# Alternating the last mixture products of a fused recurrence and mixer between two PSUM banks

## The chip, the cores and the metric

The kernel runs on one core of one Trainium2 chip. The metric is the device time of one execution in microseconds (us), from the profiler on the chip. A core has five engines with a queue of instructions each: TensorE (PE: matmuls, their weight loads are PEld), VectorE (DVE), ScalarE (ACT), GpSimd (POOL) and SyncE (SP, which here issues nearly all DMAs). Each engine takes its own queue strictly in order and waits for the others through semaphores. Matmuls write to PSUM, which has eight banks of 2 KB per partition; DVE and ACT read it.

## What is computed

A recurrence over 768 steps for 4 batches of 8 heads, and a gated mixer over its output:

```
for t in range(S):                                   # S = 768, state 40 x 40 per head
    y[t]  = r[t] @ state
    Sa    = state @ a[t]
    state = state * w[t] - outer(Sa, b[t]) + outer(v[t], k[t])
x = y as [batch, S, 320]
h = relu(x @ w_in)                                   # 320 -> 1024
u, v = h[..., :512], h[..., 512:]
v_n = (v - mean(v)) / sqrt(var(v) + 1e-6)
v_s = einsum('ts,bsd->btd', w_spatial, v_n) + b_spatial[:, None]
out = (u * v_s) @ w_out                              # 512 -> 320
```

## The kernel before

There are two phases in one program. **Phase 1** goes through the recurrence in NS = 24 chunks: two pairs of batches (bq = 0, 1) with twelve chunks of 64 steps each. Every chunk has a chain of small matmuls (c_bp L535, c_ff L553, c_xx L571, c_mp L603, c_y L627) with ACT copies and POOL masks between them, and every fourth chunk gets the inverses of its blocks from `invert`, whose temporary, itmp, is a PSUM tile that DVE writes and reads. Each second chunk ends with 128 finished steps stored to the DRAM buffer xs.

Beside the recurrence phase 1 computes `relu(x @ w_in)`. For each of twelve tiles j (a pair of batches and 128 steps) it loads x (`m_load`, L670 and L674), splits it into two float32r parts xh and xl (`m_split`: ACT, then POOL L54) and runs six **products** of eight matmuls each: four of `m_u` (L739; a slice of u for both batches, 128x256) and two of `m_v` (L694; the v half for one batch, 128x512). ACT takes each product out of PSUM with the Relu (L741 for u, L696 for v). u goes to the DRAM buffer uts. v is normalised first (`m_n1`, `m_root`, `m_n2`, `m_n3`: DVE, POOL, ACT) and then goes to vns. I number the products k = 0 to 71 in the program's order; every third (50, 53, ..., 71) is an `m_v`. The tiles xh, xl, ur and vr have two buffers each. All products use one PSUM tile, pv, in the pool ps_m with one buffer.

**Phase 2** is the mixer over the steps. For each batch b and each half h of its steps, `spatial(b, h)` makes four PSUM tiles pg (d = 0 to 3; 18 matmuls each, L173 to L175); DVE adds the bias (L177) and multiplies by u (L178, tile ut, loaded from uts at L158), and ACT and POOL split the result into gh and gl. `proj` multiplies these by w_out: three tiles po of 12 matmuls (L193), one half behind `spatial`. The tiles gh, gl and g have two buffers, pg has four, po three. The buffers vh, vl of v (loaded at L149 into raw) and ut alternate between two sets; the set for b = 1 and 3 lies in SBUF where phase 1's xh, xl, ur and vr lie.

The order: `plan` is a list of pieces with due times in chunks, and the part before time 24 is written in this order under manual_schedule. The pieces from time 24 on, which I call the **tail** (products 52 to 71), and all of phase 2 are put in order by the framework's scheduler, which sets them between each other and the last chunks. So the order on each queue is fixed when the program is built.

Of the kernel before, what the change touches and what calls it, by code (L numbers as in the profile page):

```python
# [8 lines left out]
F32 = mybir.dt.float32  # L9
# [6 lines left out]
PSUM = bass.MemoryType.PSUM  # L16
DRAM = bass.MemoryType.DRAM

P = 128
# [4 lines left out]
NB = 2  # L24
# [7 lines left out]
DH = 512  # L32

@with_exitstack
def tile_kernel(ctx, tc, early, late, vtok, win, wspT, bsp, wout, out):
    nc = tc.nc
    dram = ctx.enter_context(tc.tile_pool(name="dram", bufs=1, space=DRAM))
    B = out.shape[0]
    S = out.shape[1]
    xs = dram.tile([B, 2, NP, E, S], F32, name="xs")  # L40
    vns = dram.tile([B, S // P, P, DH], F32, name="vns")
    uts = dram.tile([B // NB, S // P, DH // P, P, NB, P], F32, name="uts")
    with ExitStack() as c1:
        phase1(c1, tc, early, late, vtok, win, xs, vns, uts, dram)
    with ExitStack() as c2:
        phase2(c2, tc, vns, uts, wspT, bsp, wout, out)
# [165 lines left out]
def phase1(ctx, tc, early, late, vtok, win, xs, vns, uts, dscr):  # L212
    nc = tc.nc
    NS = early.shape[1]
# [6 lines left out]
    def pool(name, bufs=1, **kw):  # L221
        return ctx.enter_context(tc.tile_pool(name=name, bufs=bufs, **kw))
# [10 lines left out]
    moe = pool("moe")  # L233
    ps_k = pool("ps_k", 2, space=PSUM)
    ps_c = pool("ps_c", 2, space=PSUM)
    ps_i = pool("ps_i", 1, space=PSUM)
    ps_b = pool("ps_b", 1, space=PSUM)
    ps_m = pool("ps_m", 1, space=PSUM)

    warm = const.tile([P, 1], F32, name="warm")  # L240
# [442 lines left out]
        split_lo(LO_ENG, xh[64:, 2], xt[64:, 2], xh[64:, 2])  # L683
        st["xhl", key] = (xh, xl)

    def m_v(g, bq, i):
        xh, xl = st["xhl", (bq, i)]
        pv = ps_m.tile([P, DH], F32, name="pv")
        vc = slice(DH, 2 * DH)
        mm = [(xh[:, k, g, :], wh[:, k, vc]) for k in range(3)]  # L690
        mm += [(xh[:, k, g, :], wl[:, k, vc]) for k in range(3)]
        mm += [(xl[:, k, g, :], wh[:, k, vc]) for k in range(2)]
        for j, (l, r) in enumerate(mm):
            nc.tensor.matmul(pv, lhsT=l, rhs=r, start=(j == 0), stop=(j == len(mm) - 1))  # L694
        vr = st["act"].tile([P, DH], F32, name="vr", bufs=2)
        nc.scalar.activation(vr, pv, AF.Relu)  # L696
        st["vr", g] = vr
# [30 lines left out]
        nc.scalar.activation(vr, vr, AF.Identity, bias=q[:, 2:3], scale=q[:, 1:2])  # L728
        nc.sync.dma_start(out=vns[bq * NB + g, i], in_=vr)

    def m_u(d, bq, i):
        xh, xl = st["xhl", (bq, i)]
        dc = slice(d * P, (d + 1) * P)
        pu = ps_m.tile([P, NB, P], F32, name="pv")
        mm = [(wh[:, k, dc], xh[:, k]) for k in range(3)]
        mm += [(wh[:, k, dc], xl[:, k]) for k in range(2)]
        mm += [(wl[:, k, dc], xh[:, k]) for k in range(3)]
        for j, (l, r) in enumerate(mm):
            nc.tensor.matmul(pu, lhsT=l, rhs=r, start=(j == 0), stop=(j == len(mm) - 1))  # L739
        ur = st["act"].tile([P, NB, P], F32, name="ur", bufs=2)  # L740
        nc.scalar.activation(ur, pu, AF.Relu)  # L741
        nc.sync.dma_start(out=uts[bq, i, d], in_=ur)
# [4 lines left out]
    def at(t, fn, *args):  # L747
        plan.append((t, len(plan), fn, args))
# [4 lines left out]
    v, p = nc.vector, nc.gpsimd  # L753
# [48 lines left out]
    for q in range(GS, NS):  # L802
        t = PREP.get(q, q - 8 + 0.01)
# [20 lines left out]
            at(T_DEC + i + k * 0.12 - (0.9 if k == 0 else 0), step, gen)  # L824
    at(T_DEC + 5.9, open_act)
    slots = [T_MOE + k // 4 + (M1, M2, M3, M4)[k % 4] for k in range(3 * NS)]
    for j in range(NS // 2):
        bq, i = j // 6, j % 6
        own = slots[6 * j:6 * j + 6]
        at(max(own[0] - 1.6, 2 * j + 2.1, T_DEC + 5.92), m_load, bq, i)  # L830
        at(max(own[0] - 0.7, 2 * j + 2.7), m_split, bq, i)
        for t, d in zip((own[0], own[1], own[3], own[4]), range(DH // P)):
            at(t, m_u, d, bq, i)
        for t, g in zip((own[2], own[5]), range(NB)):
            at(t, m_v, g, bq, i)
            at(t + 0.14, m_n1, g)
            at(t + 0.42, m_root, g)
            at(t + 0.48, m_n2, g)
            at(t + 0.76, m_n3, g, bq, i)
# [12 lines left out]
    with tc.manual_schedule():  # L852
# [77 lines left out]
        while plan[n][0] < NS:  # L930
            t, _, fn, args = plan[n]
# [59 lines left out]
```

## Time and profile before

| | us |
|---|---|
| median of three runs | 725.92 (725.43 to 728.48) |
| profiled execution, its own time | 728.03 |
| profiled execution, span from first to last instruction | 726.2 |
| PE busy in the span | 592.8 (82%) |
| DVE, ACT, POOL busy | 448.6, 415.1, 289.7 |

The page gives the mean granted clock of PE as 0.901 of full speed. In the page's 40 slices of 18.2 us PE is at nine tenths or more from the 23rd slice to the 39th, but for the 26th with an 8 and the 35th with a 5. The matmul groups at L173, L174 and L175 (pg) have 192 matmuls each and the longest busy times of PE, 65.1, 65.0 and 64.8 us.

How to read it: a busy share is a mean over stages with different bounds. So the windows of the end of the program are read apart, and for each the question is which wait ended last there.

### The profile page before, as it was taken

Reading aid. Unit: us, or ns where it says so; the run is one execution under the profiler, and the core shown is the slowest. Engines: PE = TensorE matmul, PEld = TensorE weight load, DVE = VectorE, ACT = ScalarE, POOL = GpSimd, SP = SyncE. Lnnn points to the kernel's source line nnn. Section 1 sums busy time; section 2 is a strip of 40 time slices with the busy share of each in tenths; the row PEclk is TensorE's granted clock in tenths of the full one; section 3 lists DMA queues with packets and bytes.
Section 4 is the critical chain, followed back from the end, with each engine's and each line's share of the span. In section 5 each row is a group of like instructions: output and inputs, shape, how many; then the busy total and the mean of one; then the engine's idle time right before and its main releaser. Section 6 shows DMA issues by size and latency. Waiting matters only on the chain. (4 is left out here: it accounts for less than half of the span.)

```text
span 726.2 us, 25447 instructions
## 1 busy us (share of the span) xinstructions
PE 592.8 (82%) x10784; PEld 535.0 (74%) x10784; DVE 448.6 (62%) x884; ACT 415.1 (57%) x904; POOL 289.7 (40%) x486
## 2 busy tenths in 40 slices
PE   2707776587776877989988999899999999599997
PEld 1606665586665776868877788788789998499997
DVE  7898689968999998758797565311247201343221
ACT  2406763377655666878878798798754423332112
POOL 4102230124433435354554543464549822373221
PEclk9956997578977888989999999999899999799999
DMA  9443675294444535454365344344263533650001
GB/s 186 86 90 69 104 145 112 51 185 94 106 91 101 112 82 118 112 126 112 102 187 165 85 133 127 106 120 116 73 198 108 158 108 100 189 180 34 28 28 55
DMA packets 101337, 81.35 MB, mean 112 GB/s; under 512 B 33576, under 2 KB 90152, under 8 KB 99304
## 3 DMA queue, kind: packets, MB, share of 16 engines
q1 hardware_dynamic: 100680, 78.01, 43.3%
q10 hardware_dynamic: 544, 1.72, 1.1%
q8 instruction: 85, 1.39, 0.9%
q14 instruction: 28, 0.23, 0.1%
HBM read 59.20 MB, written 20.50 MB: 110 GB/s over the span
## 5 line engine op out<-in xcount | busy, mean ns | idle before, releaser
L396 POOL TENSOR_SCALAR_AFFINE_SELECT Rt<-Rt 64x512 f32<-64x512 f32 (+1 forms) x144 | 84.1, 585 | 102.2 <-ACT Rt L582 74.4
L545 ACT ACTIVATE Rt<-bp 64x416 f32<-64x416 f32 x96 | 49.1, 512 | 68.2 <-PE bp L535 66.4
L351 DVE TENSOR_TENSOR itmp<-A 128x30 f32<-128x30 f32 (+9 forms) x180 | 73.7, 409 | 3.3
L396 POOL TENSOR_SCALAR_AFFINE_SELECT At<-At 64x512 f32<-64x512 f32 x48 | 36.9, 768 | 94.6 <-ACT At L406 92.5
L173 PE MATMUL pg<-wsh,vh 128*128 128x384 f32 x192 | 65.1, 339 | 0.0
L174 PE MATMUL pg<-wsl,vh 128*128 128x384 f32 x192 | 65.0, 339 | 0.0
L175 PE MATMUL pg<-wsh,vl 128*128 128x384 f32 x192 | 64.8, 337 | 0.0
L355 DVE TENSOR_TENSOR A<-A,itmp 128x30 f32<-128x30 f32 (+9 forms) x180 | 59.0, 328 | 6.2
L535 PE MATMUL bp<-lin,Mc 40*64 40x104 f32 x768 | 53.1, 301 | 11.1 <-DVE y L640 10.3
L535 PEld LDWEIGHTS bp<-lin,Mc 40*64 40x64 f32 x768 | 46.2, 167 | 16.0 <-DVE y L640 13.4
L177 DVE TENSOR_TENSOR g<-pg,bb 128x384 f32<-128x384 f32 x32 | 17.7, 553 | 63.9 <-PE pg L175 56.9
L702 DVE BATCH_NORM_STATS2 bs<-vr 128x6 f32<-128x512 f32 x24 | 16.6, 690 | 60.3 <-ACT vr L696 60.2
L54 POOL TENSOR_TENSOR gl<-g,gh 128x384 fp32r<-128x384 f32 x32 | 33.8, 1062 | 47.7 <-ACT gh L50 47.7
L582 ACT ACTIVATE Rt<-ch 64x416 f32<-64x416 f32 x96 | 49.2, 512 | 3.9 <-PE ch L571 1.5
L326 PE MATMUL bk<-at,sl 64*32 64x32 f32 x1536 | 24.4, 221 | 28.6 <-DVE sl L313 14.5
L553 PE MATMUL ch<-Rt,At 128*64 128x104 f32 x768 | 46.0, 277 | 1.2 <-issue 1.2
L50 ACT ACTIVATE gh<-g 128x384 fp32r<-128x384 f32 x32 | 16.7, 522 | 52.3 <-DVE g L178 52.3
L441 PE MATMUL bk<-ident,sl 128*128 128x128 f32 x192 | 31.7, 297 | 17.4 <-ACT tk L447 6.9
L553 PEld LDWEIGHTS ch<-Rt,At 128*64 128x64 f32 x768 | 40.3, 152 | 5.7 <-issue 3.0
L326 PEld LDWEIGHTS bk<-at,sl 64*32 64x32 f32 x1536 | 20.6, 132 | 30.7 <-DVE sl L313 14.6
L571 PE MATMUL ch<-ffs,xf 64*64 64x104 f32 x768 | 42.6, 263 | 0.0
L54 POOL TENSOR_TENSOR vl<-raw,vh 128x512 fp32r<-128x512 f32 x24 | 32.1, 1350 | 25.8 <-ACT vh L50 24.8
(121 smaller groups left out, 1604.2 us busy)
## 6 DMA issues: line engine op xcount, KB each, us to landing
ein<-in_early SPq DMA_DIRECT2D x40, 387.0 KB
lin<-in_late SPq DMA_DIRECT2D x48, 160.0 KB
uts<-ur SPq DMA_DIRECT2D x48, 128.0 KB
vns<-vr SPq DMA_DIRECT2D x24, 256.0 KB
raw<-vns SPq DMA_DIRECT2D x24, 256.0 KB
ut<-uts SPq DMA_DIRECT2D x24, 256.0 KB
Rt<-in_vtok SPq DMA_DIRECT2D x48, 80.0 KB
xs<-y SPq DMA_DIRECT2D x48, 80.0 KB
```

Source lines behind the costliest of these rows:

```text
L54: eng.tensor_tensor(out=lo, in0=x, in1=hi.bitcast(F32), op=ALU.subtract)
L173: nc.tensor.matmul(pg, lhsT=vh[:, dc], rhs=w_h, start=(i == 0), stop=False)
L174: nc.tensor.matmul(pg, lhsT=vh[:, dc], rhs=w_l, start=False, stop=False)
L175: nc.tensor.matmul(pg, lhsT=vl[:, dc], rhs=w_h, start=False, stop=(i == NT - 1))
L326: nc.tensor.matmul(pl[o:o + HB, n, :], lhsT=sl[PR[par], n, par, cs], rhs=at[PR[par], n, cs], start=True, stop=True,)
L351: nc.vector.tensor_tensor(out=tp, in0=A[:, k + 1:, k:k + 1].broadcast_to([P, m, k]), in1=A[:, k:k + 1, 0:k].broadcast_to([P, m, k]), op=AL ...
L355: nc.vector.tensor_tensor(out=A[:, k + 1:, 0:k], in0=A[:, k + 1:, 0:k], in1=tp, op=ALU.add)
L396: nc.gpsimd.affine_select(out=t, in_=t, pattern=[[0, k], [1, C]], base=0, channel_multiplier=-1, compare_op=ALU.is_gt, fill=0.0,)
L535: nc.tensor.matmul(bp[PR[par], q, :], lhsT=Mc[RR[par], n, :], rhs=li[RR[par], n, C:], start=(q == 0), stop=False, skip_group_check=True,)
L545: nc.scalar.activation(Rt[par][PR[par], gp, :], st["bp", g][PR[par]], AF.Copy)
L553: nc.tensor.matmul(ff[PR[1 - par], q, :], lhsT=At[par][:, n, :], rhs=Rt[par][:, n, :], start=True, stop=True,)
L582: nc.scalar.activation(Rt[par][PR[par], gp], xx[PR[1 - par]], AF.Copy, scale=-1.0)
```

## The change

Three edits. The pool ps_b now stands ahead of ps_i, so that ps_b gets PSUM banks 4 and 5 (before: 5 and 6), and ps_i, the pool of the inversion's itmp, gets bank 6 (before: 4); ps_m keeps bank 7. In phase 2 the pool of po takes banks 4, 6 and 5, in this order, before and now. A helper m_ps hands out ps_m's tile for an even k and a tile named itmp in ps_i for an odd one. And products of the tail get their number as k, while all others keep k = 0; so products 53, 55, ..., 71 write bank 6, the other ten of the tail bank 7.

```diff
     ps_c = pool("ps_c", 2, space=PSUM)
+    ps_b = pool("ps_b", 1, space=PSUM)
     ps_i = pool("ps_i", 1, space=PSUM)
-    ps_b = pool("ps_b", 1, space=PSUM)
     ps_m = pool("ps_m", 1, space=PSUM)
...
-    def m_v(g, bq, i):
+    def m_ps(k):
+        return ps_i.tile([P, DH], F32, name="itmp") if k % 2 else ps_m.tile([P, DH], F32, name="pv")
+
+    def m_v(g, bq, i, k=0):
         xh, xl = st["xhl", (bq, i)]
-        pv = ps_m.tile([P, DH], F32, name="pv")
+        pv = m_ps(k)
...
-    def m_u(d, bq, i):
+    def m_u(d, bq, i, k=0):
...
-        pu = ps_m.tile([P, NB, P], F32, name="pv")
+        pu = m_ps(k)[:, 0:NB * P].rearrange("p (g t) -> p g t", g=NB)
...
     slots = [T_MOE + k // 4 + (M1, M2, M3, M4)[k % 4] for k in range(3 * NS)]
+
+    def tail(t):
+        return slots.index(t) if t >= NS else 0
+
...
-            at(t, m_u, d, bq, i)
+            at(t, m_u, d, bq, i, tail(t))
...
-            at(t, m_v, g, bq, i)
+            at(t, m_v, g, bq, i, tail(t))
```

The scheduler makes another order of it on every engine. Three places matter. Lines after the helper have moved by three (L739 is now L742, L694 is L697, L729 is L732).

The first is PE in chunk 22. Before, a u product (three rows of pv) stands ahead of the chain's matmuls L477 and L419, and these stand ahead of the sixteen matmuls of c_mp (L603), which nothing interrupts:

```order
L571 MATMUL ch<-ffs,xf_130 64x104 x16
L739 MATMUL pv<-xh,wh 128x256 x3
L739 MATMUL pv<-xl,wh 128x256 x2
L739 MATMUL pv<-xh,wl 128x256 x3
L477 MATMUL bk<-XT_7493,l_8438 32x32 x16
L419 MATMUL bk<-lin_137 64x64 x16
```

Now, at the same place and a little further, between the two halves of c_mp:

```order
L742 MATMUL pv<-xh,wl 128x256 x3
L697 MATMUL itmp<-wh,xh 128x512 x2
L477 MATMUL bk<-XT_7493,l_8438 32x32 x16
L419 MATMUL bk<-lin_137 64x64 x16
L603 MATMUL ch<-tk,Rt_132 40x40
```

```order
L603 MATMUL ch<-tk,Rt_133 40x40
L697 MATMUL itmp<-wh,xh 128x512
L697 MATMUL itmp<-wl,xh 128x512 x3
L697 MATMUL itmp<-wh,xl 128x512 x2
L603 MATMUL ch<-tk,Rt_132 40x40
```

Product 53, the second v product of tile j = 8, has moved here from behind product 52, past six other products; two of its matmuls stand ahead of L477, six between the halves of c_mp.

The second is PE at the end of the tail. Before, products 65, 66, 67 and 68 (and then 69, 70 and 71) follow each other with nothing between them, behind the tile pg_9881 of spatial(1, 1) and behind 72 matmuls po:

```order
L175 MATMUL pg_9881<-wsh_9276,vl_9518 128x384
L694 MATMUL pv<-wh,xh 128x512 x3
L694 MATMUL pv<-wl,xh 128x512 x3
L694 MATMUL pv<-wh,xl 128x512 x2
L739 MATMUL pv<-xh,wh 128x256 x3
L739 MATMUL pv<-xl,wh 128x256 x2
L739 MATMUL pv<-xh,wl 128x256 x3
L739 MATMUL pv<-xh,wh 128x256 x3
```

Now, the last two products, 70 and 71:

```order
L175 MATMUL pg_9744<-wsh_9246,vl_9488 128x384
L742 MATMUL pv<-xh,wh 128x256 x3
L742 MATMUL pv<-xl,wh 128x256 x2
L742 MATMUL pv<-xh,wl 128x256 x3
L173 MATMUL pg_9744<-wsh_9252,vh_9493 128x384
L174 MATMUL pg_9744<-wsl_9253,vh_9493 128x384
L175 MATMUL pg_9744<-wsh_9252,vl_9494 128x384
L173 MATMUL pg_9744<-wsh_9258,vh_9499 128x384
L174 MATMUL pg_9744<-wsl_9259,vh_9499 128x384
L175 MATMUL pg_9744<-wsh_9258,vl_9500 128x384
L697 MATMUL itmp<-wh,xh 128x512 x3
L697 MATMUL itmp<-wl,xh 128x512 x3
```

From product 65 on, pieces of 4 to 16 matmuls pg stand between one product and the next but for one pair, 65 and 64, which are nested in each other. The last product has moved ahead of the last 9 matmuls of pg_9744, of pg_9857, pg_9881 and of all 72 matmuls po, which now follow it.

The third is SP at the loads of ut for b = 1 (ut_9521). Before:

```order
L742 DMA uts<-ur 128x256 x2
L729 DMA vns<-vr 128x512
L742 DMA uts<-ur 128x256 x2
L729 DMA vns<-vr 128x512
L158 DMA ut_9804<-uts 128x4x128
L158 DMA ut_9521<-uts 128x4x128 x6
```

Now:

```order
L745 DMA uts<-ur 128x256 x2
L732 DMA vns<-vr 128x512
L745 DMA uts<-ur 128x256
L149 DMA raw<-vns 128x512
L158 DMA ut_9521<-uts 128x4x128 x6
L158 DMA ut_9804<-uts 128x4x128
```

The six loads still stand behind the stores of products 68 and 70. A load of v (raw) has come ahead of them, and the last part of ut_9804 (for b = 2) now follows them.

## The prediction

> **What bounds the kernel now.** I read the granted clock and PE's busy share in windows first, then PE's waits in the end of the program, then the chain of waits there. The first view has the window, its length, then busy us of PE, PEld, DVE, ACT and POOL with their counts, the granted clock, DMA share and GB/s:
>
> ```profile
> 510.00:515.00 5.00, 4.86 (x118) 4.31 (x118) 0.00 (x0) 4.89 (x12) 1.79 (x3) 1.00 0.24 83
> 515.00:520.00 5.00, 3.52 (x96) 3.05 (x92) 2.50 (x5) 4.50 (x11) 4.73 (x7) 0.76 0.38 104
> 520.00:525.00 5.00, 4.99 (x42) 3.61 (x42) 0.44 (x2) 1.47 (x4) 2.53 (x9) 0.56 0.08 32
> 560.00:580.00 20.00, 20.00 (x127) 19.62 (x126) 4.86 (x10) 7.85 (x18) 17.15 (x28) 1.00 0.54 157
> 580.00:600.00 20.00, 19.55 (x117) 18.54 (x116) 2.52 (x6) 5.87 (x13) 5.84 (x11) 1.00 0.30 98
> 609.50:624.10 14.60, 11.13 (x58) 8.23 (x56) 2.08 (x6) 4.54 (x10) 3.75 (x15) 1.00 0.26 87
> 624.10:631.30 7.20, 0.02 (x1) 0.02 (x1) 2.07 (x5) 2.21 (x5) 1.39 (x7) 0.69 0.95 262
> 631.30:637.20 5.90, 5.90 (x21) 5.90 (x22) 3.88 (x5) 1.97 (x4) 5.06 (x5) 0.51 0.59 192
> 650.00:670.00 20.00, 20.00 (x123) 20.00 (x122) 6.01 (x10) 4.98 (x10) 7.90 (x7) 1.00 0.27 93
> ```
>
> PE is full from 520 to the end, but for 0.45 us in 580 to 600, for 3.47 us (14.60 less 11.13) while the last seven products run, and for a hole of 7.2 us behind them. After the hole its clock is at half for 6 us. So from 520 on, time is PE's work plus these gaps, and work that leaves PE's queue or a gap that closes shortens the kernel one for one. The waits of PE between 608 and 640:
>
> ```profile
> PE po L193 <- ACT gh L50: 7.2, 1, 7.2
> PE pv L739 <- ACT vr L696: 1.4, 2, 0.7
> PE pv L694 <- ACT ur L741: 1.0, 2, 0.5
> PE pv L739 <- ACT ur L741: 1.0, 2, 0.5
> ```
>
> The last three are the one bank: each product waits for the Relu of the one ahead. The chain shows what the hole is:
>
> ```profile
> 607.68 0.95 PE pv L739 x8
> 608.98 0.17 PE pg L175
> ...
> 609.68 1.87 PE pv L694 x8
> ...
> 612.23 1.23 PE pv L739 x8
> 615.71 2.13 PE pv L694 x8
> 621.54 0.39 ACT ur L741
> 621.95 1.69 DMA uts<-ur
> 623.73 0.37 SPq L158
> 625.31 4.72 DMA ut<-uts
> 630.11 0.57 DVE g L178
> 631.28 4.37 PE po L193 x15
> 635.65 0.32 PE pg L173
> 657.98 0.18 PE pg L175
> 658.16 5.29 PE po L193 x36
> ```
>
> The u of batch 1 lies where xh and xl lay, so its six loads start behind the last product (624.1), and DVE's multiply gets its data at 630.11. By then PE has used up pg's four buffers and all po, and stands.
>
> **The change part by part.** The sum is made against the profiled execution, 728.03 us (span 726.2 and 1.8 around it).
>
> *Waits between products, −3.5.* A product now waits for the Relu of the one two ahead, and by the new order 4 to 16 matmuls pg of 0.17 us lie between. The 3.47 us go. The Relus stay as long and lie beside PE's work.
>
> *First matmuls, −1.6.* A u product takes 1.23 behind a wait and 0.95 behind a pg, a v product 2.13 and 1.87: four times 0.28 and two times 0.26.
>
> *The hole, −7.2, and its half clock, −2.9.* What now stands behind the last product on PE's queue is 45 matmuls pg (9 of pg_9744, 18 of pg_9857, 18 of pg_9881) at 0.175 and 72 po at 5.29/36 = 0.147, together 18.5 us. The loads need 6.2 us from the last product to DVE's multiply (623.9 to 630.1). So the wait moves under work that stood ahead of it before; 12 us of cover are left. Without a hole the clock stays: 15 po in 4.37 would take 2.2, the five pg 1.6 at the row's 0.32 would take 0.9.
>
> *Product 53, −1.9, and its place, +0.6.* One v product leaves the full stretch and goes into chunk 22, where PE waits for ACT:
>
> ```profile
> 514.62 0.72 POOL L54 TENSOR_TENSOR xh<-xt,xh 64x256 fp32r<-64x256 f32 x1
> ...
> 516.28 0.51 PE L603 MATMUL ch<-tk,Rt 128*40 128x40 f32 x16 [0.40 <-ACT Rt L582]
> 517.85 0.77 PE L603 MATMUL ch<-tk,Rt 128*40 128x40 f32 x16 [1.07 <-ACT Rt L582]
> ```
>
> Its data are split at 515.34 (514.62 + 0.72), ahead of the place. Two matmuls ahead of L477 push c_mp's first half by 0.1 or so, as 0.40 of it is waiting. The other six (about 1.5) start at 516.8, and the second half, ready at 517.85, starts about 0.5 late. Queued behind them are c_mp, L504, product 47 and c_y of the same chain, so this delay counts whole. Bounds: 0 (it fits the gaps) and 2.0 (at half clock). I take 0.6.
>
> *The half clock of 517.8 to 525, −2.5.*
>
> ```profile
> 499.82 0.69 PE bk L504 x32
> 505.04 2.04 PE pv L694 x8
> 518.63 1.06 PE bk L504 x32
> 519.70 3.71 PE pv L694 x8
> 523.41 1.53 PE bp L627 x32
> ```
>
> After 1.47 us of waits PE ran at half clock: L504 lost 0.37, product 47 lost 1.67, and L627 about 0.5 by L504's ratio. With product 53 in the gap PE is as full as in 510 to 515 (4.86 of 5, clock 1.00), the nearest row, so I take the whole 2.5; the other end is 0. The Trainium skill, "TensorE: Matmul & The Clock Gate", Part 1, says that the clock halves after at least one idle window of about 3.4 us. By it gaps of 1.07 us would cost nothing and this term would be 0; here the rows show half clock behind just such gaps, so the measurement decides.
>
> *New stalls, +2.0.* In 547 to 601 PE now runs 18 products instead of ten, and behind each Relu, store and split other work queues on ACT and SP. The trace of before has 0.45 us of stalls for its ten; by the count that is 0.8 for eighteen. The upper end is the price that the last products paid, 0.5 to 0.7 for each of some twelve, 7 us. I take 2.0, nearer the row of the same stretch.
>
> *The pool order* costs no instruction. It puts the second po tile on the products' bank 6, so `proj` can't finish ahead of product 71; the work that hides it is pg, 164 matmuls between 547 and the last product (28.5 us). The slice of the bank for u has the same shape as before: nothing.
>
> Sum: −3.5 −1.6 −7.2 −2.9 −1.9 +0.6 −2.5 +2.0 = −17.0. From the profiled 728.0 that is 711.0. The median of the runs is 2.1 lower, about what one half-clocked stretch like that of 517.8 costs; a run without it would not gain the 2.5, and comes out at 725.9 − 14.5 = 711.4. I predict **711**.
>
> **The rivals.**
>
> *The hole stays (A).* The loads of u stand behind a load of raw, which needs the store of product 68's v. If that store is late by over 12 us, PE runs dry again and pays 10.1: 721. For it: v's chain can be slow. These ACT rows are a Relu (L696) and the same tile's last step (L728), and a wait for raw:
>
> ```profile
> 554.95 0.58 ACT L696 ACTIVATE vr<-pv 128x512 f32<-128x512 f32 x1
> 568.95 0.82 ACT L728 ACTIVATE vr<-vr,q 128x512 f32<-128x512 f32 x1
> 585.83 0.63 ACT L50 ACTIVATE vh<-raw 128x512 fp32r<-128x512 f32 x1 [4.74 <-DMA raw<-vns]
> ```
>
> It took 14 us there. Against it: POOL was 17.15 of 20 busy then, and 5.84 of 20 from 580 on.
>
> *The bank is not what products wait for (B).* The two buffers of vr bind instead: a v product's Relu needs the store of the one two ahead, and the products stop in PE's queue as before. The first two terms are lost: 716. With A it is 726, no change. Against it: v products now come 8 to 9 us apart, so a chain of 14 and a store of 2 just fit.
>
> *Slower (C).* ACT is in order, and between the Relus of products 60 to 70 it now takes five splits of v (L50) that wait for a load or for PE's last use of the buffer. Where one stands for 4.74 us as above, both banks fill and PE, two products later, stands too. In before this happened once, and cost PE 0.45. From four such full stalls on (19 us) the gain is gone and more: 711 + 19 = 730. Against it: PE needs two products and 2 to 5 us of pg to notice.
>
> *The clock swings (D).* The trace's seven products with gaps of 0.5 to 0.7 us kept clock 1.00 (609.5 to 624.1). So small gaps alone don't do it; if they did now, eighteen products (twelve of 0.95, six of 1.87: 22.6 us) at half clock would give 711 + 22.6 = 734. The Trainium skill, same page, "A second HAM failure mode: psum-queue depth-cycling", speaks for this: cycling through PSUM banks makes PE idle briefly and its clock oscillate. No run so far bears it out.
>
> **How the numbers follow.** Forecast 0.70 (705.5 to 717), A or B alone 0.14 (716 to 722), A and B 0.08 (726), C 0.06 (730), D 0.02 (734). A measurement can tell about 0.5% from no change, 3.6 us: under 722.3 is faster. So faster 0.83, same 0.09, slower 0.08. The forecast's lower end is 711 − 5.5: no stalls (−2.0), no delay in chunk 22 (−0.6), the lower runs (−0.5) and 2.4 if the clock's dips elsewhere go too. The upper: stalls of 7 (+5) and 0.8 of delay. To hold 8 in 10 the range reaches into A: 705.5 to 720.
>
> **What would show it.** PE's windows: full from 510 to the end, with no hole of over 2 us, and clock 1.00 from 520 on. The last product ends near 598 to 603 instead of 624.1, and DVE's multiply with batch 1's u stops waiting for a DMA that PE feels. The po of batch 0 run after the last product. A wait of PE for gh (A), of products for vr or ur (B), or ACT's waits for raw with PE idle two products later (C) would show the rivals. Most harmful to the forecast would be stalls between 560 and 600 that add up to over 7 us.

## The result, and the profile after

The changed kernel takes 705.61 us (median of four runs: 700.41, 705.23, 705.99, 706.29) beside 725.67 for the kernel before in the same measurement. The ratio is 0.9682, 95% interval 0.9648 to 0.9716: faster, by more than forecast. The ratio is not the quotient of these two medians, which is 0.9724. The median stands at the lower end of the range; by the ratio it is 702.8 us for a before of 725.92, which is below it. The comparisons leave out the slow executions, of the kernel before three of 55 (730.88, 735.7 and 736.44 us). Two later measurements of the same changed kernel gave 0.9804 (0.9756 to 0.9853) and 0.9774 (0.9727 to 0.9821). The first interval and the second don't overlap; why that is became the main question.

The profiled execution took 706.29 us, span 704.4, mean granted clock 0.912 (before 0.901). The same windows as before, after the change (window, length, busy us of PE, PEld, DVE, ACT and POOL, granted clock, DMA share, GB/s):

```profile
510.00:515.00 5.00, 5.00 (x121) 4.14 (x115) 2.44 (x5) 4.46 (x11) 4.73 (x7) 1.00 0.31 95
515.00:520.00 5.00, 4.92 (x64) 4.10 (x63) 1.63 (x4) 3.07 (x6) 2.77 (x10) 1.00 0.23 84
520.00:525.00 5.00, 5.00 (x53) 3.97 (x51) 0.16 (x1) 2.02 (x5) 0.95 (x5) 1.00 0.42 120
560.00:580.00 20.00, 19.08 (x115) 17.62 (x113) 6.14 (x13) 9.57 (x20) 16.80 (x31) 1.00 0.57 173
580.00:600.00 20.00, 18.90 (x114) 18.19 (x114) 3.68 (x10) 6.75 (x15) 5.74 (x19) 1.00 0.50 155
600.00:610.00 10.00, 9.68 (x65) 9.36 (x64) 4.71 (x8) 5.10 (x12) 5.96 (x11) 1.00 0.79 245
610.00:620.00 10.00, 10.00 (x61) 10.00 (x60) 3.49 (x6) 2.50 (x5) 5.44 (x5) 1.00 0.23 75
```

The clock is 1.00 from 510 to 703, behind PE's last instruction, and there is no hole. What PE lacks from 560 to 610 is 2.34 us, and PE's waits from 505 to the end name all of it:

```profile
PE itmp L742 <- ACT vr L699: 1.1, 1, 1.1
PE pv L697 <- ACT ur L744: 0.9, 1, 0.9
PE po L193 <- ACT ot L194: 0.3, 1, 0.3
```

These are the new stalls, forecast at 2.0. Product 71 ends at 593.37 instead of 624.1, and the first po starts at 597.22. (With the 5.02 us that this execution is ahead, as shown below, that is 598.4, within the 598 to 603 of the forecast.) Behind 610 PE has no gap to its last instruction.

The place in chunk 22, PE's timeline after (start, us, line, operands, count, and in brackets the idle time before it, of which there is none here):

```profile
509.55 0.69 PE L477 MATMUL bk<-XT,l 32*32 32x32 f32 x32
510.17 1.15 PE L419 MATMUL bk<-lin 40*64 40x64 f32 x32
511.25 0.51 PE L603 MATMUL ch<-tk,Rt 128*40 128x40 f32 x16
511.69 0.50 PE L697 MATMUL itmp<-wh,xh 128*128 128x512 f32 x1
512.02 0.85 PE L697 MATMUL itmp<-wl,xh 128*128 128x512 f32 x3
512.71 0.61 PE L697 MATMUL itmp<-wh,xl 128*128 128x512 f32 x2
513.25 0.51 PE L603 MATMUL ch<-tk,Rt 128*40 128x40 f32 x16
513.69 0.69 PE L504 MATMUL bk<-zt,X 32*32 32x32 f32 x32
```

Six matmuls of product 53 fill the gap between the halves of c_mp, neither half waits, and L504 takes 0.69 instead of 1.06. So every step that the prediction would see in the trace is there. But c_xx (L571) of chunk 22 starts at 506.37 (its line stands below, with e5's) where it started at 511.39 before:

```profile
511.39 1.64 PE L571 MATMUL ch<-ffs,xf 64*64 64x104 f32 x32
```

So 5.02 us were gained ahead of it, where the order of the instructions is the same in both kernels and the forecast counted nothing. From there to the end of the span it is 214.8 before and 198.0 after, 16.8 less; the forecast for this part was 17.0.

That gives two theories. **W**: the stretch ahead of chunk 22 wanders from execution to execution, with nothing changed. **X**: the change makes it faster in some way that the order doesn't show.

### The profile page after: what moved, and what is told of

The parts are those of the page before. It is cut to its first block, busy times and chain, and to the rows that moved or that the text cites. A ratio compares the mean times of both kernels' runs of the same rounds, so it can differ in the third digit from the quotient of the medians.

```text
span 704.4 us, 25450 instructions
## 1 busy us (share of the span) xinstructions
PE 585.0 (83%) x10784; PEld 529.8 (75%) x10784; DVE 447.6 (64%) x884; ACT 413.5 (59%) x904; POOL 291.1 (41%) x486
## 5 line engine op out<-in xcount | busy, mean ns | idle before, releaser
L396 POOL TENSOR_SCALAR_AFFINE_SELECT At<-At 64x512 f32<-64x512 f32 x48 | 38.4, 801 | 93.5 <-ACT At L406 91.3
L535 PE MATMUL bp<-lin,Mc 40*64 40x104 f32 x768 | 51.6, 297 | 10.7 <-DVE y L640 10.2
L571 PE MATMUL ch<-ffs,xf 64*64 64x104 f32 x768 | 43.1, 263 | 0.3 <-issue 0.3
```

Of the source, the lines that this page charges most:

```text
L396: nc.gpsimd.affine_select(out=t, in_=t, pattern=[[0, k], [1, C]], base=0, channel_multiplier=-1, compare_op=ALU.is_gt, fill=0.0,)
L535: nc.tensor.matmul(bp[PR[par], q, :], lhsT=Mc[RR[par], n, :], rhs=li[RR[par], n, C:], start=(q == 0), stop=False, skip_group_check=True,)
```

## The experiments

Each profile is cut at c_xx of chunk 22 (the last landmark with the same order ahead of it) and of chunk 23. The cuts are the start times of L571 in PE's timeline, the rest is the span less these; the last two columns are from the runs.

| kernel | c_xx of chunk 22 at | from there to the end | of it to chunk 23 | of it behind | median | ratio |
|---|---|---|---|---|---|---|
| before | 511.39 | 214.8 | 23.87 | 190.9 | 725.67 | |
| e1, only the pool order | 510.45 | 213.1 | 23.86 | 189.2 | 725.19 | 1.000 |
| e2, before again | 509.08 | 213.5 | 22.93 | 190.6 | 727.27 | 1.002 |
| e7, u of batch 1 elsewhere | 509.68 | 210.8 | 23.90 | 186.9 | 723.0 | 0.996 |
| after | 506.37 | 198.0 | 21.47 | 176.6 | 705.61 | 0.968 |
| e3, after again | 509.58 | 196.8 | 21.50 | 175.3 | 709.06 | 0.980 |
| e5, after, third time | 515.05 | 197.1 | 21.49 | 175.6 | 706.7 | 0.977 |
| e8, after, u elsewhere | 510.95 | 197.0 | 21.48 | 175.5 | 709.33 | 0.975 |
| e9, after, old pool order | 512.71 | 197.4 | 21.49 | 175.9 | 709.31 | 0.977 |
| e4, product 53 in its place | 508.12 | 200.3 | 23.89 | 176.4 | 710.46 | 0.983 |
| e6, last twelve alone | 504.90 | 200.4 | 22.91 | 177.5 | 714.12 | 0.987 |
| e10, from chunk 20 on | 508.85 | 203.1 | 23.91 | 179.1 | 714.69 | 0.985 |

**e1: the pool order alone**, with no alternation; the instructions stand in the same order as before on every engine.

```
     ps_c = pool("ps_c", 2, space=PSUM)
+    ps_b = pool("ps_b", 1, space=PSUM)
     ps_i = pool("ps_i", 1, space=PSUM)
-    ps_b = pool("ps_b", 1, space=PSUM)
```

> The kernel before with only the PSUM pools in the new order (ps_b in banks 4 and 5, itmp in bank 6); every instruction stands where it stood before. Theory W (the 5.0 us that the changed kernel had gained in its profile ahead of chunk 22 are the wandering of PE's half-clocked stretches from one execution to the next): the time is that of the kernel before, 725 to 728.5, and the first matmul of c_xx in chunk 22 starts anywhere in 506 to 513, while the stretch from there to the end takes 214.8 within 2.5. Theory B (the banks themselves make phase 1 faster): 720 to 722, with c_xx of chunk 22 at 506.4 within 1, and each chunk earlier by about the same share.

Measured: 725.19, ratio 1.0 (0.9965 to 1.0036). The banks by themselves change nothing that these runs can tell. Its profile shows more: from c_xx of chunk 12 to that of chunk 13 it takes 18.26 us (319.02 to 337.28), where before took 22.74 (315.51 to 338.25) for the same instructions. Before's windows there (columns as above):

```profile
320.00:325.00 5.00, 2.38 (x68) 2.16 (x68) 2.14 (x6) 1.67 (x4) 1.95 (x3) 0.81 0.64 113
325.00:330.00 5.00, 5.00 (x113) 4.55 (x114) 2.11 (x7) 1.22 (x4) 0.69 (x4) 0.51 0.28 58
```

Before's waits of PE from 315.5 to 338.2 (waiting line, what it waited for, us in total, times, longest; "issue" is nothing that the profile shows):

```profile
PE bk L504 <- issue: 2.6, 1, 2.6
```

The windows of the same place in e1:

```profile
323.50:328.50 5.00, 4.92 (x177) 4.26 (x176) 3.78 (x12) 2.90 (x8) 2.01 (x4) 1.00 0.78 138
328.50:333.50 5.00, 4.62 (x81) 3.93 (x82) 4.79 (x11) 3.85 (x8) 1.18 (x6) 1.00 0.50 111
```

And e1's waits of PE there, from 319 to 337.3:

```profile
PE bp L535 <- issue: 0.5, 1, 0.5
```

In before PE stood for 2.6 us in front of L504, waiting for nothing that the profile shows, and then ran at half clock. In e1 there was neither. This is one place where an execution gets or loses 4.5 us without any change in its instructions.

**e2: the kernel before, with nothing edited.**

> The kernel before, a second profile of it. Theory W: c_xx of chunk 22 starts over 1 us away from the 511.4 of the first profile, though nothing differs; the stretch from there to the end is again 214.8 within 2.5. Theory B: it starts at 511.4 within 1, and the runs lie at 725.7 within 1.

Measured: 727.27, ratio 1.0019 (0.998 to 1.0059), with single runs from 718.36 to 730.75. c_xx of chunk 22 starts at 509.08, 2.31 us earlier than in the first profile. W holds at this size.

**e3: the changed kernel again, with nothing edited.**

> The changed kernel, a second profile of it. Theory W: c_xx of chunk 22 starts over 1 us away from 506.4, the stretch from there to the end takes 198.0 within 2, and the runs spread by 4 us or more. Theory B: 506.4 within 1 again, runs within 1.5 of 705.6.

Measured: 709.06, ratio 0.9804 (0.9756 to 0.9853). c_xx of chunk 22 starts at 509.58, 3.21 us later than in the first profile of the same kernel, and the stretch behind it is 196.8. The gain behind the landmark is there again, the one ahead of it is not.

**e4: product 53 stays on the first bank**, so it keeps its old place; the alternation begins with product 54.

```
     def tail(t):
-        return slots.index(t) if t >= NS else 0
+        return slots.index(t) if t >= slots[54] else 0
```

> The changed kernel with the alternation from product 54 on, so that product 53 stays on pv and behind product 52; chunk 22 is as before. If the prediction's three terms for product 53 hold (1.9 of PE's work out of the full stretch, 0.6 of delay, 2.5 for the half clock that it keeps off), the stretch from c_xx of chunk 22 to the end is 198.0 + 3.8 = 201.8 and the half clock is back between 517 and 525. The rival, that the half clock falls there or not by chance of the execution: 199.3, clock 1.00, or half clock in some other place.

Measured: 710.46, ratio 0.9828 (0.9782 to 0.9875), stretch 200.3, between the 201.8 of the three terms and the 199.3 of the rival. The half clock is back where the terms had it. Beside the mean of the changed kernel's order, 197.3, three us of the gain are product 53's, not 3.8. Its windows show where:

```profile
510.00:515.00 5.00, 3.54 (x101) 3.11 (x101) 1.52 (x3) 4.79 (x12) 4.84 (x5) 0.96 0.12 33
515.00:520.00 5.00, 4.98 (x50) 3.60 (x46) 0.99 (x2) 1.38 (x3) 4.05 (x12) 0.50 0.31 105
```

And c_mp with its waits, and L504 behind it, in e4's timeline of PE:

```profile
513.01 0.51 PE L603 MATMUL ch<-tk,Rt 128*40 128x40 f32 x16 [0.40 <-ACT Rt L582]
514.58 0.76 PE L603 MATMUL ch<-tk,Rt 128*40 128x40 f32 x16 [1.06 <-ACT Rt L582]
515.36 1.06 PE L504 MATMUL bk<-zt,X 32*32 32x32 f32 x32
```

The two gaps are back, and the half clock behind them. From chunk 22 to chunk 23 it takes 23.89, and 21.47 to 21.50 in all five profiles with product 53 in the gap, though there eight matmuls more run in it. Behind chunk 23 e4 takes 176.4 beside 175.3 to 176.6: product 53's own 1.9 us are partly covered by fewer stalls (1.0 beside 1.5 to 2.3); some 0.5 of them is not accounted for.

**e5: the changed kernel a third time**, on another chip.

> The changed kernel once more, nothing edited. Theory W (the size from chunk 22 on is fixed, about 16.6 us; what stands ahead of it wanders from execution to execution with nothing changed): the stretch from the start of c_xx of chunk 22 to the end of the span takes 196.5 to 198.5 (198.0 and 196.8 in the two profiles so far), chunk 22's c_xx starts anywhere from 506 to 511, and the median lies between 704 and 711, ratio 0.972 to 0.982. Rival X (the change itself makes the part ahead of chunk 22 faster, as the first measurement had it): c_xx of chunk 22 starts at 506 to 507 again and the ratio is 0.972 or less.

Measured: 706.7, ratio 0.9774 (0.9727 to 0.9821), stretch 197.1 as expected. c_xx of chunk 22 starts at 515.05, even outside the 506 to 511 that W was given, and this profiled execution took 714.0. The earliest and the latest start of it in the four profiles with the changed kernel's order, from PE's timeline of after and then of e5:

```profile
506.37 1.64 PE L571 MATMUL ch<-ffs,xf 64*64 64x104 f32 x32
```

```profile
515.05 1.65 PE L571 MATMUL ch<-ffs,xf 64*64 64x104 f32 x32
```

X falls: the eight profiles with an alternation reach chunk 22 anywhere from 504.9 (e6) to 515.05, with a mean of 509.6; the four without it from 509.1 to 511.4, with a mean of 510.2.

**e6: alternation for products 60 to 71 only**, with the line of e4 and slots[60].

> Alternation only for products 60 to 71 (the others stay on the one bank, so product 53 keeps its old place and the pg spread thinner between the products). In the order, products 60 to 71 stand nearly in a row, and 72 matmuls po, 10.6 us, stand behind product 71. Theory (the hole goes because enough work of batch 0 stands behind the last product, more than the 6.2 us that the loads of u need; products in a row do not wait with two banks): no hole, the last products cost under 1.5 us of waits, but the half clock at c_mp of chunk 22 stays; the stretch from c_xx of chunk 22 to the end takes 200 to 202, as with product 53 in its place (200.3), ratio 0.981 to 0.986. Rival (products that stand in a row wait in spite of two banks, for ACT): twelve times 0.55, so 206 to 208, ratio 0.99.

Measured: 714.12, ratio 0.9871 (0.9816 to 0.9926), stretch 200.4 as the theory had it; the ratio is just above its bounds. PE's waits from 515 to the end:

```profile
PE pv L742 <- ACT vr L699: 1.6, 1, 1.6
PE pv L697 <- ACT ur L744: 0.2, 1, 0.2
```

Twelve products nearly in a row cost 1.8 us of waits (under 1.5 were expected) where seven in a row on one bank cost 3.47, and no hole follows them: 10.7 us of po stand behind product 71 (602.56 to 613.27). So for the hole it is enough that work of batch 0 stands behind the last product, whichever it is.

**e7: before's one bank, with batch 1's u in another place in SBUF**; the PSUM pools are as before.

```
-    up = [pool("ua", 1), None]
+    up = [pool("ua", 1), pool("ub", 1)]
...
-    up[1] = pool("ub", 1)
```

> Before's one bank and its order of the PSUM pools, but the pool of batch 1's u is opened ahead of the pools p2s and p2w, so that u no longer lies where phase 1's xh and xl lie; its loads needn't wait for the last product. The scheduler then puts products 62 to 71 in a row, with more of the pg behind them. Theory (the hole is these loads and nothing else): hole and its half clock go (10.1), while ten products with one bank in a row wait 0.55 each and pay 0.27 each for a first matmul behind a wait, 3 us more than before's seven paid: the stretch from c_xx of chunk 22 to the end takes 206 to 208 (before 213.8), ratio 0.989 to 0.992. Rival (another buffer of phase 2 then lies there and waits in u's place): the hole stays, 213 to 217, ratio 1.0 or more.

Measured: 723.0, ratio 0.9958 (0.992 to 0.9996), stretch 210.8. It lies between the theory (206 to 208) and the rival (213 to 217). PE's waits from 580 to 615:

```profile
PE pv L694 <- ACT ur L741: 2.1, 4, 0.5
PE pv L739 <- ACT ur L741: 2.1, 4, 0.5
PE pv L739 <- ACT vr L696: 2.1, 3, 0.7
PE pg L173 <- ACT vh L50: 1.4, 2, 1.2
```

The hole and its half clock are gone, so they were the loads of this u. But eleven products in a row now wait 6.3 us for the one bank, not the 5.5 of ten, pg waits 1.4 for the splits of v, which was not foreseen, and each product pays for its first matmul. By these rows the gain should be about 5 us (10.1 for the hole, less 2.8 and 1.4, less four first matmuls of 0.27); it was 2.3 to 4.0 against the three profiles with before's order. The remaining 1 to 2.5 us are open. A freed load alone is worth little here, since the scheduler then packs the products closer.

**e8: the same move of u on the changed kernel.**

> The changed kernel with the same move of batch 1's u. Theory (the change has already hidden the loads wholly; freeing them again is worth nothing): the stretch from c_xx of chunk 22 to the end takes 196 to 199 (196.8 and 198.0 in the two profiles of the changed kernel), ratio within 0.003 of that of the changed kernel in this job. Rival (the two moves add up): 190 or less. Rival (products 66 to 71 in a row without pg between them wait again): 200 to 202.

Measured: 709.33, ratio 0.9754 (0.9698 to 0.9811), stretch 197.0. The loads were already hidden wholly; freeing them again is worth nothing, and e7's and the change's gains don't add up, because they are the same hole.

**e9: the alternation with the old pool order**, so that the products' second bank is that of the first po tile.

```
     ps_c = pool("ps_c", 2, space=PSUM)
-    ps_b = pool("ps_b", 1, space=PSUM)
     ps_i = pool("ps_i", 1, space=PSUM)
+    ps_b = pool("ps_b", 1, space=PSUM)
```

> The alternation with before's order of the PSUM pools, so that products of odd number write bank 4, which is also the bank of the first po tile (the changed kernel: bank 6, that of the second). The order of the instructions is that of the changed kernel on every engine. Theory (po stands behind product 71 and 23 matmuls pg anyway, so it makes no difference which po bank the product shares): the stretch from c_xx of chunk 22 to the end takes 196.5 to 198.5, ratio 0.972 to 0.982. Rival (the first po has to wait for the Relu of product 71 and its release, which the second po does not feel): a wait of po of over 1 us, stretch 199 to 201.

Measured: 709.31, ratio 0.9772 (0.9724 to 0.982), stretch 197.4, and no wait of po at all. The change of the pool order is not needed.

**e10: the alternation from chunk 20 on**, with the line of e4 and 20.2 in place of slots[54].

> The alternation begins with the products of chunk 20 instead of the tail's first. Product 53 stands behind product 52 again, out of chunk 22's gap. Theory (the gain of product 53's place was the cover of that gap, and products in the recurrence don't wait for their bank): the half clock at c_mp of chunk 22 is back and the stretch from c_xx of chunk 22 to the end takes 199.5 to 201.5, as with product 53 in its place (200.3), ratio 0.976 to 0.986. Rival (products of chunks 20 to 23 gain from a second bank as the tail's did): 197 or less, and chunk 20 to chunk 22 shorter than the 36.4 to 36.5 that all profiles show.

Measured: 714.69, ratio 0.9854 (0.9802 to 0.9905), stretch 203.1, 1.6 above the theory's bounds; chunk 20 to chunk 22 took 36.48, as in before, so the products there gain nothing from a second bank. The half clock in chunk 22 is back. What was not foreseen is a second one, in the tail; e10's only wait of PE from 522 to the end:

```profile
PE pv L742 <- ACT vr L699: 2.1, 1, 2.1
```

And its windows around this wait:

```profile
575.00:580.00 5.00, 2.89 (x19) 2.57 (x18) 1.39 (x4) 2.06 (x6) 4.06 (x4) 1.00 0.36 112
580.00:585.00 5.00, 5.00 (x26) 5.00 (x26) 1.61 (x6) 2.38 (x6) 4.30 (x8) 0.66 0.75 222
```

One stall of 2.1 us, and then 3.4 us at half clock (580.2 to 583.6; the five us have a mean of 0.66), which cost 1.7. Stalls of 1.1 (after) and 1.6 (e3, e6) left the clock at 1.00.

No kernel tried is measurably faster than the changed one; e8's ratio is the lowest of the later ones, but its stretch is the same.

## Why the prediction came out as it did

**The mechanism and the sum were right for what lies behind c_xx of chunk 22.** There the four profiles with the changed kernel's order (after, e3, e5, e9) take 196.8 to 198.0, mean 197.3; the three with before's order (before, e1, e2) 213.1 to 214.8, mean 213.8. That is 16.5 us; the terms' sum was 17.0.

- *Waits between products, the hole and its half clock, first matmuls, product 53's own time, new stalls*: together −15.1 forecast for what lies behind chunk 23, −14.4 measured (190.2 to 175.8). The new stalls are 2.3 in after and 1.5 to 1.7 in e3, e5 and e9 (forecast 2.0).
- *Product 53's place and the half clock of chunk 22*: −1.9 forecast (−2.5 + 0.6), −2.1 measured (23.55 to 21.49). Against before and e1, whose half clock lasts 6.8 us (in e2 it is 3.4), it is −2.4, so the place itself costs about 0.1, not 0.6: the second half of c_mp starts 6.88 us behind c_xx instead of 6.46 (513.25 − 506.37, 517.85 − 511.39), as forecast, but L504 starts 7.32 behind it instead of 7.24. It starts 7.24 behind it in e2 too, where this half ran at full clock and L504 then stood 0.28 for ACT's zt (516.32 − 509.08). So most of the delay falls into time in which L504 waits anyway. The Trainium skill, "TensorE: Matmul & The Clock Gate", Part 1, asks for an idle window of about 3.4 us ahead of a half clock; by it this term would have been 0. e4, with gaps of 0.40 and 1.06, and e10, with one of 2.1, show half clock behind shorter idle times, so the measurement decides.
- *The pool order costs nothing*: so e1 and e9.
- *The rivals.* A: no hole in any kernel with the alternation. B: its mechanism came, but in one place and small. The stall of 1.1 us of after (1.6 in e3, 1.3 in e5, 0.9 in e9; 1.6 in e6 and 2.1 in e10 are of the same kind) is a u product that waits for the Relu of a v product, and this Relu itself stood 2.5 to 3.2 us for the store of an earlier vr (first row below). C: it came too; PE's other wait for a Relu, 0.9 in after and 0.6 in e9, stands behind a split of v that waited for raw (second row). D: the clock is 1.00 through the tail of after, with its products on two banks in turn. ACT's timeline in after, with its wait in brackets:

```profile
580.45 0.60 ACT L699 ACTIVATE vr<-itmp 128x512 f32<-128x512 f32 x1 [2.53 <-DMA vns<-vr]
563.74 0.63 ACT L50 ACTIVATE vh<-raw 128x512 fp32r<-128x512 f32 x1 [1.90 <-DMA raw<-vns]
```

**What failed is the step from the sum to a time.** "From the profiled 728.0 that is 711.0" puts everything ahead of chunk 22 at no change. In the first profile of the changed kernel that part was 5.02 us shorter, and in e3, e5 and e9 it was 1.81 shorter, 3.66 longer and 1.32 longer than in the one profile of before, with the instructions in the same order. The second working of the time had a fault of its own. The prediction said: "The median of the runs is 2.1 lower, about what one half-clocked stretch like that of 517.8 costs; a run without it would not gain the 2.5, and comes out at 725.9 − 14.5 = 711.4." The stretch is no accident of the profiled run: all seven profiles that keep product 53 out of the gap (before, e1, e2, e4, e6, e7, e10) show half clock behind the same two gaps, and chunk 22 takes 22.9 to 23.9 in them. So the whole 17.0 had to come off the median too, which gives 708.9, and the difference between the profiled execution and the median was something else.

That something is the spread of the executions, which the range's lower end has as "the lower runs (−0.5)" and 2.4 "if the clock's dips elsewhere go too". Three runs of before, from 725.4 to 728.5, were taken as its spread. Its executions in fact go from 717.9 to 730.2 (the 52 that the comparisons of four measurements use), because the part ahead of chunk 22 is not fixed: in twelve profiles whose instructions up to there stand in the same order it takes 504.9 to 515.05. The changed kernel's 16 runs go from 700.4 to 714.0. Their mean is 707.8 (standard deviation 3.4), before's 725.0: 17.2 us, with twice the standard error of these means about 1.9. This agrees with the sum of 17.0. The first measurement's four runs lie 3.3 under that mean, and its interval, from four runs, was narrower than the spread between measurements. So the change is worth about 2.3% (16.5 to 17.2 of 725), and the rest of the first 3.2% lies with the executions that were measured; whether that was luck alone or something that differed in that measurement, no run shows.

So the forecast of 711 was 3 us too high for the changed kernel's mean: its one working began at an execution 3.0 us above the mean of before (728.03, 725.0), and its other left out 2.5 us without cause. And the range left too little room, 2.9 us, for where the executions of the part that isn't changed happen to fall. What sets that in each execution was not tried, but the twelve profiles show where it lies. Chunks 17, 18, 20 and 21 take the same time in all of them within 0.1 us. The stand in front of L504 of chunk 12 is in ten of them, with 1.8 to 2.8 us, and only e1 and e6 lack it. Stands of over 0.6 us for which the profile shows no cause ("issue") are all ahead of 328 us: 11 to 16 in each profile, 20.7 to 32.2 us together. After, the second earliest at chunk 22, has 23.3 us of them, and e5, the latest, 32.2; but e4, with the fewest, is only third, so they explain it in part. Why PE stood there is open. From chunk 13 to 21 only chunks 16 and 19 differ by over 1 us between profiles, and there it is half clock that follows the same gap or doesn't (last section).

## What to carry to other kernels

Before a gap between one profiled execution and a median is explained by one event, look whether that event is in every execution; and take the spread from landmarks of a second profile, not from three times. Where a load waits for a buffer that earlier work holds, it helps to let other work stand behind the last user of that buffer, and this can come from a quite different edit, like a second PSUM bank that lets the scheduler move the last products forward. A small piece of work without a deadline can be worth more than its own time in a gap of the critical chain: there product 53 cost the chain about 0.1 us, the half clock stayed away, and the move was worth 3 us for 1.9 us of work.

## What the runs showed of the hardware

Half clock followed quite short idle times of PE, but not by their length alone. Gaps of 0.40 and 1.07 us with 0.5 us of work between them, in c_mp of chunk 22, were followed by it in all seven profiles that had them, for 6.8 us in five and for 3.4 in e2 and e6; a single stall of 2.1 us as well (e10, for 3.4 us). Single stalls of 1.1 and 1.6 us in the tail were not, and neither were e7's eleven of 0.5 to 0.7 us in a row and a twelfth of 1.2: the clock in its windows from 580 to 610 is 1.00.

Even the same gap did both. In chunk 16 all twelve profiles have one of 1.06 or 1.07 us in c_mp. Half clock follows it for 3.4 us in eight of them, for 6.8 us in three (after, e3, e6) and not at all in e4, and the chunk takes 20.0 to 20.2, 21.1 to 21.4 and 18.7 us. PE's timeline of e3 and then of e4:

```profile
401.74 0.51 PE L603 MATMUL ch<-tk,Rt 128*40 128x40 f32 x16 [1.07 <-ACT Rt L582]
402.52 1.06 PE L504 MATMUL bk<-zt,X 32*32 32x32 f32 x32 [0.28 <-ACT zt L486]
```

```profile
402.92 0.51 PE L603 MATMUL ch<-tk,Rt 128*40 128x40 f32 x16 [1.06 <-ACT Rt L582]
403.70 0.69 PE L504 MATMUL bk<-zt,X 32*32 32x32 f32 x32 [0.28 <-ACT zt L486]
```

So a half clock in one profile says little; that of chunk 22 counts because seven profiles of seven have it, and none of the five without the gaps. And the same instructions in the same order reach the same landmark up to 10 us apart (504.9 to 515.05).
